# A long convolution and an MLP on one core: another order of issue, more buffers, reads and loads on other queues, half of y formed in the front, MLP rows turned by transfers

## The chip, the cores and the metric

One core of a Trainium2 chip runs the whole program. The metric is the device time of one execution in microseconds (us); lower is better. TensorE is PE (its weight loads PEld), VectorE is DVE, ScalarE is ACT, GpSimd is POOL and SyncE is SP. SP and POOL issue the transfers here; each takes its issues in the order of its program, and a wait of one holds up what stands behind it.

## What is computed

x is 2048 x 512 in bf16. A state-space layer filters the normed x along the 2048 rows, each of 512 channels with a filter of its own made from 128 complex modes (Uf and Kf are the spectra of the padded rows and filter); a layer norm, an MLP of width 1376 and two residual sums follow.

```python
def _A_ref(u, A_re, A_im, B_re, B_im, C_re, C_im, log_dt, Dskip):
    ...
    P = jnp.exp(logdA[:, :, None] * l[None, None, :])
    K = jnp.einsum("dn,dnl,dn->dl", Cc, P, dB).real
    ...
    Yf = Uf * Kf[None, :, :, :]
    ...
    y = y.transpose(0, 2, 1) + u * Dskip[None, None, :]
    return y

def _B_ref(x, w1, b1, w2, b2):
    y = _layernorm(x, axis=-1)
    h = _gelu(jnp.einsum("bsd,df->bsf", y, w1) + b1)
    return jnp.einsum("bsf,fd->bsd", h, w2) + b2

x = A_u
h = x + _A_ref(_layernorm(x, axis=-1), A_A_re, A_A_im, A_B_re, A_B_im, A_C_re, A_C_im, A_log_dt, A_Dskip)
h2 = h + _B_ref(_layernorm(h, axis=-1), B_w1, B_b1, B_w2, B_b2)
```

## The kernel before

The convolution is a Fourier product made of matmuls. In the **front**, the 16 row groups of x are normed (`norm_in`: statistics, then `roots`), and each goes through a first stage: `norm` makes `u`, two matmuls `aps`, a copy to the tile `a`, a write to `A_dram` (L786). Four loads (`x_load`, L798) bring that back in another layout as X, and `x_stage` multiplies X by the table M, in eight pairs for each half of the channels. Beside that `params`, `tables`, `exps`, `p_half`, `q_half` and `kgen` make the filter of one half of the channels (256): P and Q are phases (PE), sines (ACT) and products (DVE); `kgen` multiplies them in bursts of 128 matmuls of 20 columns (`kps`, L704), writes the filter to DRAM (`puts`, L729) and reads it back as `kt` (`gets`, L736: five reads, three of SP and two of POOL).

`conv` then goes over eight tiles k2 for a half: `spectrum` (four groups of five matmuls of 256 columns, L840, two of them led by one of two rows for the skip term, L838), a copy to `kf`, four DVE products, `back` (eight matmuls, L862 to 865), a copy to `z` (3 buffers), a write of 256 KB to `Zd` (the put, L883), and a read of it with rows and columns exchanged into `ZT` (the turned read, `turn`, L881). The second half does the same.

All of this is issued in an order written out as a list of numbers (`ORDER`): each operation of `Sched` has an index, an entry is twice the index plus the choice of engine where there are two, and every engine and queue takes its own in the order of the list. When both halves are in `ZT`, the **MLP** starts: y of a row group is two matmuls over `ZT` (by `Dm`), x is added, and `bn_stats` and `bn_aggr` give the norm. There are four tiles of four row groups. For each, `scale` norms the rows, `turn` transposes them on PE (`tps`, four 128 x 128 blocks a row group) and copies them with ACT to `y2T`, `up` runs 11 chunks of W1 with a gelu, and `down` 11 chunks of W2, adds the residual and stores. Tile 0 goes in two pairs of row groups. y of the next tile (`y_row`) stands between the up chunks, its transposes between the rows of `down`. `loads` brings W1, x and W2 from POOL in one go, once `kt` of the second half has landed: 1376, 512, 1280 and 1536 KB and some small ones. One part of y, the first half of the channels for the four rows of tile 0, is formed in the front (`early_rows`).

Of the kernel before, what the change touches and what calls it, by code (L numbers as in the profile page):

```python
# [915 lines left out]
def load_w1(nc, K, big, sb, w1, b1):  # L916
    both = big.tile([P, 4 * F + 4 * 512], bf16, name="w1_r0", tag="b2")
    K.w1_sb = both[:, 0:4 * F].rearrange("p (c f) -> p c f", c=4)
    K.r0 = both[:, 4 * F:].rearrange("p (j d) -> p j d", j=4)
    nc.gpsimd.dma_start(K.w1_sb, w1.rearrange("(dc p) f -> p dc f", p=P))  # L920
    b1_bf = sb.tile([P, NFC], bf16, name="b1_bf")
    nc.gpsimd.memset(b1_bf[:], 0.0)
    with nc.allow_non_contiguous_dma(reason="tiny bias load"):
        nc.gpsimd.dma_start(b1_bf[:, 0:10], b1[0:1280].rearrange("(fc p) -> p fc", p=P))
        nc.gpsimd.dma_start(b1_bf[0:96, 10:11], b1[1280:1376].rearrange("(p o) -> p o", o=1))
    K.b1_bf, K.b1_sb = b1_bf, sb.tile([P, NFC], f32, name="b1_sb")
# [9 lines left out]
def mlp(nc, tc, K, ZT, ov):  # L936
    with tc.tile_pool(name="m_sb", bufs=1) as sb, tc.tile_pool(name="m_rot", bufs=2) as rot, tc.tile_pool(name="m_ps", bufs=2, space=PSUM) as ps1:
        warm = sb.tile([1, 1], f32, name="warm")
        nc.scalar.activation(warm[:], K.ones[0:1, 0:1], ACT.Sqrt)
# [30 lines left out]
        def y_row(tb, jj):  # L970
            j = 4 * tb + jj
            yp = ps1.tile([P, 512], f32, name="yps")
            for h in range(2):
                nc.tensor.matmul(yp[:], lhsT=K.D[:, h], rhs=ZT[:, :, h, j, :], start=(h == 0), stop=(h == 1))  # L974
            st = rot.tile([P, 6], f32, name="st2")
            tt(nc, h_of(j), yp[:], K.r1[:, j - 4, :], ALU.add)
            nc.vector.bn_stats(st[:], h_of(j))
            nc.vector.bn_aggr(mv[tb][:, jj, :], st[:])

        def turn(tb, js):  # L980
# [29 lines left out]
        pairs = (slice(0, 2), slice(2, 4))  # L1010
        for n, js in enumerate(pairs):
            yp = yps[n] = ps1.tile([P, 2, HW], f32, name="y1", tag="yps")
            first_half(nc, K, yp, 1, js)
        tiles(1)
        at = {0: 0, 2: 1, 6: 2, 10: 3}
        for n, js in enumerate(pairs):
            first_sums(nc, K, yps[n][:], 1, js)
            for jj in range(js.start, js.stop):
# [149 lines left out]
```

## Time and profile before

| | |
|---|---|
| median of 3 runs | 339.08 us (338.14 to 341.11) |
| span of the profiled execution | 340.1 us |
| PE busy | 253.5 us, 75% |
| DVE busy | 203.8 us, 60% |
| ACT busy | 188.0 us, 55% |
| POOL busy | 32.6 us, 10% |
| moved by DMA | 30.18 MB, mean 89 GB/s |

The profile is of one execution. A busy time says how long an engine had an instruction in work; a wait is put down to what ended it last. A chain is followed back from the last instruction to what released each step, so its shares say which work or transfer set the end. The granted clock is that of TensorE as a share of full speed (1.00 is 2.4 GHz and 0.50 is 1.2 GHz). In the rows, starts are us from the start of the span, and several instructions of one kind in a row are merged (x2).

### The profile page before, as it was taken

What the parts mean: (1) busy time and instruction counts of PE and PEld (TensorE: products, weight loads), DVE (VectorE), ACT (ScalarE), POOL (GpSimd) and SP (SyncE); (2) the same over time, 40 slices, a digit from 0 to 9 for tenths busy, and PEclk for the clock granted to TensorE, in tenths of its full rate; (3) what the DMA queues carried; (4) which work ended last, traced back from release to release, by engine and by line L of the source; (5) the groups of instructions that cost most, each with busy time, mean ns of one, the idle gap of its engine ahead of it and who ended that gap; (6) DMA issues with size and microseconds to landing.
All of it is one profiled execution on the core that took longest, in us unless ns stands there. A gap on an engine that the chain in (4) does not pass through costs nothing.

```text
span 340.1 us, 6070 instructions
## 1 busy us (share of the span) xinstructions
PE 253.5 (75%) x2408; PEld 155.3 (46%) x2422; DVE 203.8 (60%) x427; ACT 188.0 (55%) x308; POOL 32.6 (10%) x92
## 2 busy tenths in 40 slices
PE   4046984476674998998798978502689799999996
PEld 4012351242373775667666755401465344444443
DVE  3999995559981999989224443510727367274102
ACT  2799796479832999986143525420573263363440
POOL 8200007800000100000015000100000000000000
PEclk9655567579955899999599997965599999999999
DMA  6400007640156921111098964443000100100001
GB/s 180 175 2 0 4 18 195 201 147 0 65 166 169 245 67 31 45 49 35 4 239 225 337 230 125 123 124 93 0 2 0 46 17 15 47 2 31 31 11 52
DMA packets 29830, 30.18 MB, mean 89 GB/s; under 512 B 7113, under 2 KB 27594, under 8 KB 29418
## 3 DMA queue, kind: packets, MB, share of 16 engines
q1 hardware_dynamic: 27722, 23.03, 23.4%
q0 software_dynamic: 2080, 6.76, 6.4%
q8 instruction: 19, 0.31, 0.4%
q14 instruction: 9, 0.07, 0.1%
HBM read 18.58 MB, written 11.20 MB: 88 GB/s over the span
## 4 chain that ended last, share of the span: by engine, by line
PE 36%; DMA 24%; DVE 18%; ACT 12%; issue 6%; POOL 2%; SPq 1%; DVEq 0%; ACTq 0%; POOLq 0%
DMA Zd<-z 13%; PE h1ps L992 12%; PE o2ps L1004 9%; PE kps L704 5%; DMA A_dram<-a 5%; PE kfps L840 4%; DMA kt<-KD_far 3%; DVE st L761 3%; DVE Pt L70 3%; DMA KD_far<-far 2%; DVE w L70 2%; ACT a L80 2%; PE yps L974 2%; ACT y2T L80 2%; DVE Q L70 1%
## 5 line engine op out<-in xcount | busy, mean ns | idle before, releaser
L994 ACT ACTIVATE hT<-h1ps,b_sb 128x512 bf16<-128x512 f32 (+3 forms) x55 | 33.0, 603 | 28.0 <-PE h1ps L992 27.4
L992 PE MATMUL h1ps<-y2T,w_r 128*128 128x512 bf16 (+3 forms) x217 | 44.7, 350 | 2.3 <-ACT y2T L80 1.9
L840 PE MATMUL kfps<-kt,M 128*128 128x256 bf16 x320 | 42.2, 278 | 1.2 <-DMA kt<-KD_far 0.6
L1004 PE MATMUL o2ps<-w_sb,hT 128*128 128x512 bf16 (+3 forms) x183 | 39.2, 366 | 1.7 <-DVE ot L70 1.5
L840 PEld LDWEIGHTS <-M 128*128 128x128 bf16 x320 | 29.2, 99 | 10.1 <-issue 3.4
L992 PEld LDWEIGHTS <-w_r 128*128 128x128 bf16 (+1 forms) x220 | 23.0, 105 | 22.4 <-issue 4.9
L70 DVE TENSOR_TENSOR pa<-X,kf 128x1024 bf16<-128x1024 bf16 x16 | 11.1, 691 | 28.1 <-ACT kf L80 28.1
L1004 PEld LDWEIGHTS <-hT 128*128 128x128 bf16 (+1 forms) x187 | 18.1, 98 | 20.9 <-issue 1.8
L704 PE MATMUL kps<-Q,Pt 128*32 128x20 bf16 x1024 | 18.6, 221 | 11.2 <-issue 9.6
L70 DVE TENSOR_TENSOR ot<-o2ps,h_sb 128x512 bf16<-128x512 f32 (+1 forms) x13 | 8.4, 650 | 29.6 <-PE o2ps L1004 28.7
L80 ACT CAST kf<-kfps 128x1024 bf16<-128x1024 f32 x14 | 14.2, 1013 | 17.2 <-PE kfps L840 9.0
L704 PEld LDWEIGHTS <-Pt 128*32 128x32 bf16 x1024 | 17.9, 169 | 12.4 <-issue 10.5
L80 ACT CAST z<-zps 128x1024 bf16<-128x1024 f32 x15 | 15.3, 1023 | 13.6 <-DMA Zd<-z 12.8
L80 ACT CAST a<-aps 128x1024 bf16<-128x1024 f32 x15 | 15.0, 1033 | 12.2 <-DMA A_dram<-a 12.2
L70 DVE TENSOR_TENSOR Pt<-s,Pt 128x1024 bf16<-128x1024 bf16 x32 | 20.4, 691 | 1.2 <-ACT s L118 1.1
L118 ACT ACTIVATE sq<-qv 128x1024 bf16<-128x1024 int16 x20 | 20.3, 1072 | 0.0
L613 ACT ACTIVATE Pt<-th 128x256 bf16<-128x256 f32 x64 | 20.3, 405 | 0.0
L80 ACT COPY y2T<-tps 128x512 bf16<-128x512 bf16 x16 | 8.5, 584 | 17.6 <-PE tps L984 17.6
L405 POOL DMA_DIRECT2D Dp<-Dd x24 | 13.0, 546 | 43.7 <-DMA Dd<-ds 42.1
L70 DVE TENSOR_TENSOR h_sb<-yps,r 128x512 f32<-128x512 f32 x12 | 8.3, 689 | 14.8 <-PE yps L974 14.8
L777 PE MATMUL aps<-u,BD 128*128 128x512 bf16 x30 | 11.0, 473 | 8.0 <-DVE u L772 5.3
L118 ACT ACTIVATE s<-pv 128x1024 bf16<-128x1024 int16 x16 | 16.6, 1064 | 0.0
(224 smaller groups left out, 470.9 us busy)
## 6 DMA issues: line engine op xcount, KB each, us to landing
A_dram<-a SPq DMA_DIRECT2D x16, 256.0 KB, 3.0
X<-A_dram SPq DMA_DIRECT2D x4, 1024.0 KB, 6.0
Zd<-z SPq DMA_DIRECT2D x16, 256.0 KB, 3.4
ZT<-Zd SPq DMA_DIRECT2D x16, 256.0 KB, 3.4
x<-in_A_u_dram SPq DMA_DIRECT2D x4, 512.0 KB, 8.7
out_dram<-ot SPq DMA_DIRECT2D x15, 128.0 KB, 1.7
r<-in_A_u_dram POOLq DMA_DIRECT2D x1, 1536.0 KB, 15.9
w_r<-in_B_w_dram POOLq DMA_DIRECT2D x1, 1376.0 KB, 8.6
```

The source lines that it names most:

```text
L70: nc.vector.tensor_tensor(out, a, b, op)
L80: nc.scalar.copy(out, in_)
L118: nc.scalar.activation(out, v.bitcast(i16)[..., 0:2 * n:2], ACT.Sin, scale=S2PI / 65536)
L405: nc.gpsimd.dma_start(t[o::128 // cnt], bass.AP(row.tensor, row.offset + 1024 * kh, [[0, cnt], [1, 1024]]))
L613: nc.scalar.activation(K.Pt[:, k, 1, :], K.th[:, ds], ACT.Exp, scale=float(8 * k))
L704: nc.tensor.matmul(kps[32 * g:32 * g + 32, i // 8, at:at + 20], lhsT=Pt[:, :, u, c], rhs=Q[:, :, u, c], start=True, stop=True, tile_positi ...
L761: o = S.op("DVE", 2.9, roots, deps=[S.op("DVE", 0.62, lambda j=j: nc.vector.bn_stats(st[:, j, :], x[:, j, :]), [here]) for j in range(16)])
L777: nc.tensor.matmul(ps[:, h, :], lhsT=K.BD[:, h].rearrange("p a b -> p (a b)"), rhs=cell["u"][:], start=True, stop=True)
L840: nc.tensor.matmul(ps[:, k, c, :], lhsT=K.M[:, t, 2 * k2 + k, c, :], rhs=kt[:, t, :], start=(c == 1 and t == 0), stop=(t == 4))
L992: nc.tensor.matmul(pt[:fs, 0:n], lhsT=K.w1_sb[:, dc, fc * P:fc * P + fs], rhs=y2T[tb][:, dc, js, :].rearrange("p a b -> p (a b)"), start=( ...
L994: nc.scalar.activation(hT[tb % 2][:fs, fc, cols], pt[:fs, 0:n], ACT.Gelu_apprx_tanh, bias=K.b1_sb[:fs, fc:fc + 1], scale=1.0)
L1004: nc.tensor.matmul(pt[:], lhsT=h[:fs, fc, jj * P:(jj + 1) * P], rhs=K.w2_sb[:fs, fc, d], start=(fc == 0), stop=(fc == NFC - 1))
```

## The change

- **Order.** The list is new: 537 entries where there were 522. In the front, operations of P and Q stand between the 16 rows; the sign, Q-by-amp products and last-row sums come behind `roots`, the Dirichlet sums and two pieces ahead of it. The first `X` load is issued behind all writes of `a` and ahead of the filter's puts. Eleven of the 16 products of `x_stage` stand behind the first spectrum, where there were eight. In `conv` nine of the 16 copies to `kf` are DVE's, where there were two.
- **Buffers.** `a` has 4 in place of 2.
- **Skip matmul.** `top` has 128 rows, zero but for two, and the skip term is a matmul with 128 rows of ones.
- **Queues.** All five reads of `kt` are SP's. A turned read can go to POOL or SP: three are POOL's (tiles 0 and 5 of half 0, tile 0 of half 1), 13 are SP's. The end of SP's list for half 1 reads: put 1; turns 7, 6 and 2 of half 0; put 0, turn 1, put 3, put 4, a piece of x, turn 4, put 5, put 2, put 6, turn 3, turn 2, put 7, turn 5, turn 6, turn 7.
- **Loads.** W1 comes in four pieces (three of POOL, one of SP) once `kgen` of half 1 is through, x in four pieces (one of POOL, three of SP), into the room of X that the products of half 0 have left; W2 is loaded at the start of the MLP, behind the `hT` memset.
- **Half of y in the front.** For all 16 rows, the first half of y is formed and summed in the front, in four groups of one matmul block and one DVE sum each; the MLP adds the second half.
- **MLP.** Tile 0 is still transposed on PE; for tiles 1 to 3 `scale` issues a transposing transfer from SP for each row, straight from `y2` to `y2T`.

```diff
-            (nc.gpsimd if t % 2 else nc.sync).dma_start(kt[:, t, :].rearrange("p (g c) -> p g c", g=4), src)
+            nc.sync.dma_start(kt[:, t, :].rearrange("p (g c) -> p g c", g=4), src)
...
-            cell["a"] = lp.tile([P, 2, 512], bf16, name="a", tag="a", bufs=2)
+            cell["a"] = lp.tile([P, 2, 512], bf16, name="a", tag="a", bufs=4)
...
-                        nc.tensor.matmul(ps[:, k, c, :], lhsT=K.ones[0:2, :], rhs=K.top[:, ds], start=True, stop=False)
+                        nc.tensor.matmul(ps[:, k, c, :], lhsT=K.ones[:], rhs=K.top[:, ds], start=True, stop=False)
...
-        def turn(k2=k2):
-            nc.sync.dma_start(K.ZT[k2:k2 + 121:8, hh].rearrange("p h j d -> p (h j d)"), Zd[4 * k2:4 * k2 + 4].rearrange("f (q r) d -> (f q) (r d)", q=4))
+        def turn(e, k2=k2):
+            (nc.sync if e == "SP" else nc.gpsimd).dma_start(K.ZT[k2:k2 + 121:8, hh].rearrange("p h j d -> p (h j d)"), Zd[4 * k2:4 * k2 + 4].rearrange("f (q r) d -> (f q) (r d)", q=4))
...
-def first_sums(nc, K, y, hh, js):
+def half_sums(nc, K, y, hh, js):
     ds = slice(HW * hh, HW * hh + HW)
-    tt(nc, K.h0[:, js, ds], y, K.r0[:, js, ds], ALU.add)
+    tt(nc, K.h[:, js, ds], y, K.X[:, js, hh, 0:HW], ALU.add)
     for j in range(js.start, js.stop):
-        nc.vector.bn_stats(K.st0[:, j, hh, :], K.h0[:, j, ds])
...
+        nc.vector.bn_stats(K.st[:, j, hh, :], K.h[:, j, ds])
+
+
+def early_rows(nc, S, K, psp, z0, r0):
+    for n in range(4):
+        cell = {}
+        js = slice(4 * n, 4 * n + 4)
+
+        def mm(cell=cell, js=js):
+            cell["y"] = psp.tile([P, 4, HW], f32, name="y0", tag="p", bufs=PB)
+            half_rows(nc, K, cell["y"], 0, js)
+
+        m = S.op("PE", 1.0, mm, z0, acq="p")
+        K.o_early.append(S.op("DVE", 2.8, lambda cell=cell, js=js: half_sums(nc, K, cell["y"][:], 0, js), [m, r0[n]], rel=[m]))
...
+    w1v = w1.rearrange("(dc p) f -> p dc f", p=P)
+    ends = []
+    for dc in range(4):
+        ends.append(S.op(("POOL", "SP"), (0.8, 0.45), lambda e, dc=dc: (nc.gpsimd if e == "POOL" else nc.sync).dma_start(K.w1_sb[:, dc], w1v[:, dc]), deps, lat=2.5))
...
         for n in range(2):
             nc.gpsimd.memset(hT[n][96:97, NFC - 1, :], 1.0)
+        load_w2(nc, K, sb, w2, b2)
...
-                ts(nc, y2[tb][:, jj, :], h_of(4 * tb + jj), mv[tb][:, jj, 0:1], ALU.subtract, rs[:, k:k + 1], ALU.mult)
+                ts(nc, y2[tb][:, jj, :], K.h[:, 4 * tb + jj, :], mv[tb][:, jj, 0:1], ALU.subtract, rs[:, k:k + 1], ALU.mult)
+                if tb:
+                    nc.sync.dma_start_transpose(y2T[tb][:, :, jj, :], y2[tb][:, jj, :])
...
+        def y_rows(tb, n):
+            yp = yps[tb, n] = ps1.tile([P, 2, HW], f32, name="y1", tag="yps")
+            half_rows(nc, K, yp, 1, slice(4 * tb + 2 * n, 4 * tb + 2 * n + 2))
+
+        def sums(tb, n):
+            half_sums(nc, K, yps[tb, n][:], 1, slice(4 * tb + 2 * n, 4 * tb + 2 * n + 2))
+            for jj in (2 * n, 2 * n + 1):
+                nc.vector.bn_aggr(mv[tb][:, jj, :], K.st[:, 4 * tb + jj].rearrange("p h s -> p (h s)"))
...
         for n, js in enumerate(pairs):
...
+            sums(0, n)
             scale(0, js)
-            turn(0, js)
+            turn(js)
+            y_rows(1, n)
             for fc in range(NFC):
                 up(0, fc, js)
-                if n and fc in at:
-                    y_row(1, at[fc])
+            sums(1, n)
         scale(1, slice(0, 4))
...
                     up(tb, fc, slice(0, 4))
-                    if tb < 3 and fc in (1, 3, 5, 7):
-                        y_row(tb + 1, fc // 2)
+                    if tb < 3 and fc in (1, 3):
+                        y_rows(tb + 1, fc // 2)
                 if tb < 3:
+                    for n in range(2):
+                        sums(tb + 1, n)
                     scale(tb + 1, slice(0, 4))
             for jj in range(4):
                 down(tb, jj)
-                if jj == (2 if tb == 0 else 1) and tb < 3:
-                    turn(tb + 1, slice(0, 4))
...
-    K.top = cp.tile([2, 512], bf16, name="top")
+    K.top = cp.tile([P, 512], bf16, name="top")
+    nc.gpsimd.memset(K.top[:], 0.0)
...
+    def residual(e, n):
+        (nc.gpsimd if e == "POOL" else nc.sync).dma_start(K.X[:, 4 * n:4 * n + 4, :, 0:HW], xv[:, 4 * n:4 * n + 4].rearrange("p j (h d) -> p j h d", h=2))
```

## Rows read from the trace of the kernel before

**Rows 1.** The page's part 4, the chain's shares of the span, by line.
```profile
DMA Zd<-z 13%; PE h1ps L992 12%; PE o2ps L1004 9%; PE kps L704 5%; DMA A_dram<-a 5%; PE kfps L840 4%; DMA kt<-KD_far 3%; DVE st L761 3%; DVE Pt L70 3%; DMA KD_far<-far 2%; DVE w L70 2%; ACT a L80 2%; PE yps L974 2%; ACT y2T L80 2%; DVE Q L70 1%
```

**Rows 2.** Windows: stretch, its length, each engine's busy us (instructions), PEclk, DMA share, GB/s.
```profile
43.10:109.30 66.20, 40.82 (x681) 25.15 (x684) 46.45 (x88) 42.02 (x50) 12.98 (x24) 0.71 0.41 121
118.20:218.50 100.30, 87.83 (x1100) 64.45 (x1104) 62.78 (x110) 59.88 (x82) 7.37 (x13) 0.93 0.44 128
218.50:242.30 23.80, 4.00 (x27) 2.56 (x26) 7.12 (x19) 5.13 (x8) 0.98 (x2) 0.59 0.32 88
242.30:340.10 97.80, 89.64 (x480) 46.82 (x486) 43.02 (x108) 40.30 (x69) 0.00 (x0) 0.97 0.06 22
```

**Rows 3.** Waits of ACT: engine, tile, line <- what ended it: us, times, longest.
```profile
ACT z L80 <- DMA Zd<-z: 12.8, 6, 5.0
ACT a L80 <- DMA A_dram<-a: 12.2, 9, 2.5
```

**Rows 4.** The same for SP's queue.
```profile
SPq L881 <- DMA Zd<-z: 41.5, 11, 11.4
```

**Rows 5.** Timeline of SP's queue at the end of the front: start, us, issue.
```profile
229.29 0.57 SPq L883 DMA_DIRECT2D Zd<-z  x1
232.83 0.48 SPq L881 DMA_DIRECT2D ZT<-Zd  x1
```

**Rows 6.** Timeline of DVE ahead of the roots.
```profile
34.69 2.49 DVE L624 TENSOR_TENSOR Q<-Q,amp 128x1024 bf16<-128x1024 bf16 x4
```

**Rows 7.** Timeline of PE in the second half's conv.
```profile
210.66 0.27 PE L862 MATMUL zps<-pa,R 128*128 128x256 bf16 x1
...
211.42 0.27 PE L865 MATMUL zps<-pa,R 128*128 128x256 bf16 x1
...
211.63 0.28 PE L838 MATMUL kfps<-top,ones 2*128 2x256 bf16 x1
...
213.04 0.28 PE L838 MATMUL kfps<-top,ones 2*128 2x256 bf16 x1
```

**Rows 8.** Timeline of PE in kgen of half 0.
```profile
100.75 2.32 PE L704 MATMUL kps<-Q,Pt 128*32 128x20 bf16 x128 [1.13 <-issue]
```

**Rows 9.** The page's part 5: group, count | busy us, mean ns | idle before, releaser.
```profile
L80 ACT CAST z<-zps 128x1024 bf16<-128x1024 f32 x15 | 15.3, 1023 | 13.6 <-DMA Zd<-z 12.8
```

**Rows 10.** Timeline of DVE, the early sum of four rows.
```profile
219.62 1.23 DVE L70 TENSOR_TENSOR h<-y,w_r 128x1024 f32<-128x1024 f32 x1 [1.89 <-PE y L890]
...
220.88 1.41 DVE L897 BATCH_NORM_STATS2 st<-h 128x6 f32<-128x256 f32 x4
```

**Rows 11.** Timeline of PE and DVE in the MLP.
```profile
265.23 2.54 PE L1004 MATMUL o2ps<-w_sb,hT 128*128 128x512 bf16 x11 [1.52 <-DVE ot L70]
...
267.61 0.61 PE L984 MATMUL tps<-ident,y 128*128 128x128 bf16 x8
...
269.38 2.54 PE L1004 MATMUL o2ps<-w_sb,hT 128*128 128x512 bf16 x10
...
302.59 0.59 PE L974 MATMUL yps<-ZT,Dm 128*128 128x512 bf16 x2
...
306.88 1.92 DVE L66 TENSOR_SCALAR y<-h_sb,mv,r4y 128x512 bf16<-128x512 f32 x4
...
317.08 10.32 PE L992 MATMUL h1ps<-y2T,w_r 128*128 128x512 bf16 x43
...
327.24 9.71 PE L1004 MATMUL o2ps<-w_sb,hT 128*128 128x512 bf16 x55
```

**Rows 12.** DMA issues: out<-in, queue, count, KB each, median us to landing.
```profile
out_dram<-ot SPq DMA_DIRECT2D x15, 128.0 KB, 1.7
...
w_sb<-in_B_w_dram POOLq DMA_DIRECT2D x1, 1280.0 KB, 12.3
Dp<-Dd POOLq DMA_DIRECT2D x8, 128.0 KB, 4.5
...
b_bf<-in_B_b_dram POOLq DMA_DIRECT2D x1, 2.5 KB, 7.8
```

More of the change, by code (lines that the diff above doesn't have):

```diff
@@ L455, in tr @@
                 T[nm] = ps[:, n, :]
-        arrive = S2("LOAD", 0.85, lambda: None, [arrive] if arrive is not None else [])
+        arrive = S2("LOAD", 0.85 if arrive is not None else 4.4, lambda: None, [arrive] if arrive is not None else [])
         Z[pair[0]] = S2("PE", 1.75, tr, [arrive], acq="p", bias=300)
@@ L735, in gets @@
             src = near[:].rearrange("(g k) r c -> (k r) g c", g=4)[128 * t:128 * t + 128] if t < 2 else far[t - 2].rearrange("(g k) r c -> (k r) g c", g=4)
-            (nc.gpsimd if t % 2 else nc.sync).dma_start(kt[:, t, :].rearrange("p (g c) -> p g c", g=4), src)
-    p = S.op("SP", 2.0, puts, ends, rel=[ends[0]], lat=3.0)
+            nc.sync.dma_start(kt[:, t, :].rearrange("p (g c) -> p g c", g=4), src)
+    p = K.o_put = S.op("SP", 2.0, puts, ends, rel=[ends[0]], lat=3.0)
     K.o_kt[hh] = S.op("SP", 1.0, gets, [p], lat=3.0, acq="kt")
@@ L826, in conv @@
     N = [P, 2, 2, HW]
-    K.o_z, back_ops = [], []
+    K.o_z, K.o_prod, back_ops = [], [], []
     for k2 in range(8):
@@ L874, in conv @@
         x = S.op("DVE", 2.1, prod, [f] + [K.o_x[hh][k2]], acq="pa", rel=[f], bias=-1.0 * k2)
+        K.o_prod.append(x)
         S.group = f"z{hh}"
@@ L878, in conv, with half_rows @@
         e = S.op(("ACT", "DVE"), (0.94, 1.2), zout, [z], acq="z", rel=[z], bias=-1.0 * k2)
-        def turn(k2=k2):
-            nc.sync.dma_start(K.ZT[k2:k2 + 121:8, hh].rearrange("p h j d -> p (h j d)"), Zd[4 * k2:4 * k2 + 4].rearrange("f (q r) d -> (f q) (r d)", q=4))
+        def turn(e, k2=k2):
+            (nc.sync if e == "SP" else nc.gpsimd).dma_start(K.ZT[k2:k2 + 121:8, hh].rearrange("p h j d -> p (h j d)"), Zd[4 * k2:4 * k2 + 4].rearrange("f (q r) d -> (f q) (r d)", q=4))
         w = S.op("SP", 0.45, lambda cell=cell, ks=ks: nc.sync.dma_start(Zd[2 * ks.start:2 * ks.stop].rearrange("f p d -> p f d"), cell["zs"][:].rearrange("p k c d -> p (k c) d")), [e], rel=[e], lat=2.4)
-        K.o_z.append(S.op("SP", 0.45, turn, [w, K.o_turn], lat=2.8))
-def first_half(nc, K, out, hh, js):
+        K.o_z.append(S.op(("SP", "POOL"), (0.45, 0.8), turn, [w, K.o_turn], lat=2.8))
+def half_rows(nc, K, out, hh, js):
     for j in range(js.start, js.stop):
@@ L913, with load_w1, biases @@
 FSZ = [128] * 10 + [96]
[L916 to L926, printed above, removed]
+def load_w1(nc, S, K, wl, sb, w1, b1, deps):
+    w1v = w1.rearrange("(dc p) f -> p dc f", p=P)
+    ends = []
+    for dc in range(4):
+        ends.append(S.op(("POOL", "SP"), (0.8, 0.45), lambda e, dc=dc: (nc.gpsimd if e == "POOL" else nc.sync).dma_start(K.w1_sb[:, dc], w1v[:, dc]), deps, lat=2.5))
+    def biases():
+        b1_bf = sb.tile([P, NFC], bf16, name="b1_bf")
+        nc.gpsimd.memset(b1_bf[:], 0.0)
+        with nc.allow_non_contiguous_dma(reason="tiny bias load"):
+            nc.gpsimd.dma_start(b1_bf[:, 0:10], b1[0:1280].rearrange("(fc p) -> p fc", p=P))
+            nc.gpsimd.dma_start(b1_bf[0:96, 10:11], b1[1280:1376].rearrange("(p o) -> p o", o=1))
+        K.b1_sb = sb.tile([P, NFC], f32, name="b1_sb")
+        nc.gpsimd.tensor_copy(K.b1_sb[:], b1_bf[:])
+    S.op("POOL", 4.0, biases, [])
+    return ends
 def load_w2(nc, K, sb, w2, b2):
@@ L939, in mlp @@
         nc.scalar.activation(warm[:], K.ones[0:1, 0:1], ACT.Sqrt)
-        h1_sb = sb.tile([P, 12, 512], f32, name="h1_sb")
-        def h_of(j):
-            return K.h0[:, j, :] if j < 4 else h1_sb[:, j - 4, :]
         hT = [sb.tile([P, NFC, 512], bf16, name=f"hT{n}") for n in range(2)]
@@ L968, in tiles, with turn @@
             y2T[tb] = rot.tile([P, 4, 4, P], bf16, name="y2T")
[L970 to L980, printed above, removed]
+        def y_rows(tb, n):
[5 more added lines that the diff above has]
+                nc.vector.bn_aggr(mv[tb][:, jj, :], K.st[:, 4 * tb + jj].rearrange("p h s -> p (h s)"))
+        def turn(js):
             for jj in range(js.start, js.stop):
@@ L983, in turn @@
                 for dc in range(4):
-                    nc.tensor.transpose(tp[:, dc, :], y2[tb][:, jj, dc * P:(dc + 1) * P], K.ident[:])
-                evac(nc, 0, y2T[tb][:, :, jj, :], tp[:])
+                    nc.tensor.transpose(tp[:, dc, :], y2[0][:, jj, dc * P:(dc + 1) * P], K.ident[:])
+                evac(nc, 0, y2T[0][:, :, jj, :], tp[:])
         def up(tb, fc, js):
@@ L1005, in down @@
                 ot = rot.tile([P, 512 // parts], bf16, name="ot", tag="ot")
-                tt(nc, ot[:], pt[:], h_of(j)[:, d], ALU.add)
+                tt(nc, ot[:], pt[:], K.h[:, j, d], ALU.add)
                 nc.sync.dma_start(ov[j][:, d], ot[:])
@@ L1010, in mlp @@
         pairs = (slice(0, 2), slice(2, 4))
+        for n in range(2):
+            y_rows(0, n)
+        tiles(1)
         for n, js in enumerate(pairs):
[L1012 to L1018, printed above, removed]
-                nc.vector.bn_aggr(mv[0][:, jj, :], K.st0[:, jj].rearrange("p h s -> p (h s)"))
+            sums(0, n)
             scale(0, js)
-            turn(0, js)
+            turn(js)
+            y_rows(1, n)
             for fc in range(NFC):
                 up(0, fc, js)
-                if n and fc in at:
-                    y_row(1, at[fc])
+            sums(1, n)
         scale(1, slice(0, 4))
@@ L1032, in mlp @@
                     up(tb, fc, slice(0, 4))
-                    if tb < 3 and fc in (1, 3, 5, 7):
-                        y_row(tb + 1, fc // 2)
+                    if tb < 3 and fc in (1, 3):
+                        y_rows(tb + 1, fc // 2)
                 if tb < 3:
+                    for n in range(2):
+                        sums(tb + 1, n)
                     scale(tb + 1, slice(0, 4))
@@ L1111, in turn, with tail @@
         K.ZT = big.tile([P, 2, 2, 16, HW], bf16, name="ZT", tag="b1")
-    def loads():
+        K.w1_sb = big.tile([P, 4, F], bf16, name="w1", tag="b2")
+    def tail():
         work.close()
         wl = ctx.enter_context(tc.tile_pool(name="wl", bufs=1, side="right"))
-        K.h0 = wl.tile([P, 4, 512], f32, name="h0")
-        K.st0 = wl.tile([P, 4, 2, 6], f32, name="st0")
-        gate = wl.tile([P, 1], bf16, name="gate")
-        nc.gpsimd.tensor_copy(gate[:], K.kt[1][:, 4, 0:1])
-        load_w1(nc, K, big, cp, B_w1, B_b1)
-        nc.gpsimd.dma_start(K.r0, xv[:, 0:4])
-        load_w2(nc, K, wl, B_w2, B_b2)
-        K.r1 = wl.tile([P, 12, 512], bf16, name="r1")
-        nc.gpsimd.dma_start(K.r1[:], xv[:, 4:16])
-        nc.gpsimd.tensor_copy(K.b1_sb[:], K.b1_bf[:])
+        K.h = wl.tile([P, 16, 512], f32, name="h")
+        K.st = wl.tile([P, 16, 2, 6], f32, name="st0")
+    def residual(e, n):
+        (nc.gpsimd if e == "POOL" else nc.sync).dma_start(K.X[:, 4 * n:4 * n + 4, :, 0:HW], xv[:, 4 * n:4 * n + 4].rearrange("p j (h d) -> p j h d", h=2))
     S.group = None
     K.o_turn = S.op("NONE", 0.0, turn, K.o_kgen)
-    ld = S.op("POOL", 6.0, loads, [K.o_kt[1]], lat=8.0)
+    load_w1(nc, S, K, None, cp, B_w1, B_b1, [K.o_turn])
+    o_tail = S.op("NONE", 0.0, tail, [K.o_put, K.o_turn])
     part("kf0", conv, cv, psp, Zd[0], 0)
-    z0 = K.o_z
+    z0, x0 = K.o_z, K.o_prod
     part("kf1", conv, cv, psp, Zd[1], 1)
-    part("first_rows", early_rows, psp, z0 + [ld] + K.o_z[6:7])
+    r0 = [S.op(("POOL", "SP"), (0.8, 0.45), lambda e, n=n: residual(e, n), x0[2 * n:2 * n + 2], lat=3.0) for n in range(4)]
+    K.o_early = []
+    part("early", early_rows, psp, z0 + [o_tail], r0)
     S.run(ORDER)
     front.close()
-    mlp(nc, tc, K, K.ZT, out_dram.rearrange("(p j) d -> j p d", j=16))
+    mlp(nc, tc, K, B_w2, B_b2, out_dram.rearrange("(p j) d -> j p d", j=16))
     order.__exit__(None, None, None)
```

11 lines of the change are left out of this document (2 added, 9 removed), and 32 rows, old and new, of the table ORDER.

## The prediction, made before the changed kernel was run

> **What bounds the kernel now.** I read the chain that ended last first. It is cut by line, and its largest line is no engine's: the write of z to DRAM, with more writes and reads of the same kind behind it [rows 1]. So time is lost where engines stand still for transfers. To see where, I cut the span at instructions that all later work needs, in us: A, to the end of the norm's roots, 43.1; B, to the last output of the first filter half (kgen of half 0), 109.3; C, to the first spectrum matmul, 118.2; D, to the last back matmul, 218.5; E, to the first up matmul of the MLP, 242.3; F, to the end, 340.1. The reader is to see how far each engine is from full in each [rows 2]: in B DVE works 46.5 of 66.2 and PE 40.8 at a mean clock of 0.71; in D PE works 87.8 of 100.3; in E nobody works; in F PE is nearly full.
>
> The waits name what B and D lose: ACT waits 12.2 in 9 waits for an `a` buffer whose write has not landed, and 12.8 in 6 for a `z` buffer [rows 3]. SyncE's own waits give the cause of the second: 41.5 ahead of the turned read (L881), for the put just before it, 11 times [rows 4]. In SP's timeline the last tiles go put, turn, put, turn, a put 3.5 behind the turn that follows it [rows 5], long after PE had done its part.
>
> The profiled span is 340.1 and the median of the runs 339.08, 1.0 below it. My sum goes by the span, and 1.0 is taken off at the end.
>
> **A** (43.1). DVE's list sets this end. Four products of Q by amp go behind the roots: 2.5 [rows 6]. The last-row sums go behind too, the Dirichlet sums and two pieces come ahead; I take these as even. A becomes 40.6 (bounds 39 and 43.1). First on POOL stands a memset of `top`, and SP's load of `top`, the last of its loads, waits for it; nothing needs it before C: hidden.
>
> **B** (66.2). Four `a` buffers stand in place of two, and p and q work is laid between the 16 rows. If DVE never stood, its 46.5 would be the length [rows 2]. The other bound is PE. Eight matmuls of 256 columns start 0.109 apart at full clock (210.66 to 211.42 is seven steps [rows 7]); 512 columns are 0.22, and 0.44 at half clock. PE's work in B after the change, all at half clock: 16 rows x 2 x 0.44 = 14.1; p 8 x 0.88 = 7.0; q 10 x 0.86 = 8.6; phases 28 x 0.44 = 12.3; 56 transposes 6.1; kgen 4 x 2.32 + 3 x 1.13 of issue [rows 8] = 12.7; in all 60.8. Between 46.5 and 60.8 I take the middle, 53.6: the mean clock of 0.71 in B is as near to one level as to the other.
>
> **C** (8.9). All five gets of `kt` are now SP's, where POOL had two: two more issues of 0.5, as a turn's [rows 5]. The first filter matmul waits for them; meanwhile ACT has the exps of half 1 and DVE its copies of X, as before. C becomes 9.9 (bounds 8.9 and 12).
>
> **D** (100.3). From one 2-row skip matmul to the next is 1.41 (211.63 to 213.04 [rows 7]); 11 matmuls at 0.109 are 1.20. So the 128-row form saves 0.21 x 32 = 6.7 of PE. PE's list before: 16 spectra x 2.82 = 45.1, 16 backs x 0.87 = 13.9, 8 X products x 0.87 = 7.0, p and q at full clock 8.1, kgen 12.7, y of four rows 0.9; 87.7, as the 87.8 of the table. After: spectra 38.4, backs 13.9, 11 X products 9.6 (three were in B and C), p and q 8.1, kgen 12.7, half of y for all 16 rows 3.5; 86.2. The stalls were 12.6. Those by z go where a put no longer stands behind a turn that waits; I let half of all go: D becomes 92.5 (bounds 86.2, no stall, and 100.3). DVE's list, 62.8 before, grows by seven copies of kf (8.6) and one early sum (2.6), some 75: covered.
>
> SP's order decides here. Of the second half's turns three stand near behind their put and ahead of other puts (tiles 1, 4 and 2); before, 11 waits were of this kind [rows 4]. Three turns are POOL's, and what waits behind them on POOL are pieces of W1 and x, wanted only in E. W1 and x go in four pieces each, where 4.7 MB were in flight at once and one put took 11.4 to land [rows 4], against 3.5 late [rows 5].
>
> **E** (23.8). Before, SP still had three puts and four turns to send after the last back matmul. After, it is the copy of z, 1.0 [rows 9], one put, 3.5, and from the issue of the last turn (232.83 [rows 5]) to the first up matmul (242.3) 9.4 as before: 13.9. Three of the four early sums now stand on DVE behind the last product: 1.23 + 1.41 each [rows 10], 7.9 in all; the copy and the put are 4.5, and a turn as long as a put, 3.5 more, covers the rest. New beside the put is W2: its load stands on POOL behind the `hT` memset, which waits for the last back matmul. 4.7 MB in flight made a put 7.9 longer (11.4 against 3.5); by bytes 1.4 MB make it 2.4 (bounds 0 and 7.9). E becomes 16.3.
>
> **F** (97.8). The transposes of tiles 1 to 3 leave PE and ACT: 267.61 to 269.38 is 1.77 for one tile [rows 11], 5.3 for three. Half of y for 12 rows went to D: 12 x 2 x 0.109 = 2.6. The wait of 1.5 for DVE (265.23 [rows 11]) goes, because DVE's sums are done sooner. That is 9.4. W2 took 12.3 to land [rows 12] and is wanted some 16 after the first up matmul: hidden; late by as much as it lands after that.
>
> Against it stand 12 transposing transfers on SP, which no row shows. An up stage takes 10.2 (317.08 to 327.24), y 0.9 and a down stage 9.7 [rows 11]: 20.8 to the next up, which needs all four. The second pair's y starts after four of eleven chunks, at 4.1; from there to the first row of y2 it was 4.3 (302.59 to 306.88 [rows 11]), now two rows at once, 4.5, and that row 0.5: 9.1. So four transfers have 11.7 together, 2.9 each if one follows the other. Nearest is the store of `ot`, 128 KB on the same queue, 1.7; farther are `Dp`, 128 KB, 4.5, and the load of `b1`, which moves two-byte elements one by one, 7.8 [rows 12]. Bounds: 0 and 3 x (4 x 7.8 - 11.7) = 58. By the nearest row they hide; for the smaller pieces I add 2.0. Stores of `ot` queue behind them, but their data come later. F becomes 90.4.
>
> The Trainium skill's page "VectorE: DVE Perf Modes", section "The three transpose paths", gives 1309 ns for a 128x128 block through the DMA crossbar; with four blocks a row, one after another, that would be an estimate of 5.2 a row, 28 late in all, a total near 328. Its page "Advanced Engine Details and Errata", section "X-Bar Transpose (TRN2)", says that such transfers are as fast as ordinary ones; by it the total would be near 300. No row here shows either.
>
> **Sum.** 40.6 + 53.6 + 9.9 + 92.5 + 16.3 + 90.4 = 303.3; less 1.0: 302.
>
> **Rivals.** First, the change does not do what it says: only 3 of 16 turned reads are on POOL, 13 stay in one line with the puts. If waits ahead of puts still hold the `z` buffers, D and E stay: 302 + 7.8 + 7.5 = 317. For it: three such waits are left, and the last put stands behind the turn of tile 2. Against it: three are not eleven, and other issues lie between a put and its turn. 0.16, 312 to 326.
>
> Second, a transposing transfer takes what `Dp` took, 4.5, one after another: 18 - 11.7 = 6.3 late a tile, 19 in all in place of 2: 319, from 312 to 338. For it: its pieces are small; against it: the 1.7 of the store. 0.12, of which 0.02 within 1% of before. The skill's 1309 ns would lie in this case.
>
> Third, on the other side: each takes 6.6 or more, toward `b1`'s 7.8. At 6.6 a tile is 14.7 late, 44 in all: 344, slower by 1.5%; at 7.8 it is 358. Below 6.5 it is not slower. For it: no row of such a transfer; against it: `b1` was loaded while megabytes of others were in flight, and in F only stores move. 0.08.
>
> The forecast, from 289 (B and D near their lower bounds) to 318 (PE at half clock in B, few stalls gone in D), has 0.58. Below 289 stand 0.02, and 0.04 between 326 and 342 by other ways, of which 0.03 within 1%.
>
> **How the numbers follow.** About 1%, 335.7 to 342.5, is what a measurement of this kernel can tell from no change. Faster: 0.58 + 0.16 + 0.10 + 0.02 + 0.01 = 0.87. Same: 0.02 + 0.03 = 0.05. Slower: 0.08. The range 288 to 328 holds the forecast (0.58), the first rival (0.16) and most of the second (0.08): 0.82.
>
> **What would show it.** B right: ACT's waits on A_dram under 2 in sum, and the last filter output near 95. D right: 1.2 a half spectrum, no idle ahead of L838, z waits under 4. E right: one put and one turn between the last back matmul and the y of the MLP. F right: no tps in tiles 1 to 3 and no wait of PE for `y2T`. Wrong would be: PE waiting on `y2T` for more than 3 a tile (second or third rival), SP waiting over 20 at L881 ahead of puts (first), or the clock at 0.5 all through B.

## The result, and the profile after

The changed kernel takes 301.56 us (median, 298.42 to 303.06) beside 338.61 of the kernel before; the ratio is 0.886, 95% interval 0.879 to 0.894. Ratios are of fast runs alone, and of these four one (303.06) counts as slow. In a second set of runs beside the experiments it took 301.40 (ratio 0.880, 0.877 to 0.883). Forecast were 302 and a range of 288 to 328.

The profiled execution has a span of 296.5 and a time of 298.4, the shortest of the four; that of the second set took 303.9, the longest of its six. Cut as in the prediction (the end of D is taken 0.2 later here, at the end of the last back matmul, in every kernel), with the profiled execution of the second set in the last column, in us:

| | before | forecast | after | after, again |
|---|---|---|---|---|
| A to the roots | 43.1 | 40.6 | 40.4 | 40.4 |
| B to the first filter half | 66.2 | 53.6 | 52.2 | 53.6 |
| C to the first spectrum | 8.9 | 9.9 | 11.5 | 11.5 |
| D to the last back matmul | 100.5 | 92.5 | 84.7 | 87.2 |
| E to the first up matmul | 23.6 | 16.3 | 19.4 | 20.7 |
| F to the end | 97.8 | 90.4 | 88.3 | 88.4 |
| span | 340.1 | 303.3 | 296.5 | 301.8 |

That the sum came out so near is in part luck: D was forecast 8 too long (5 in the second execution) and F 2, which stands against C and E, 2 and 3 to 4 too short. The steps are taken apart below. First the windows of after, B to F, which answer to [rows 2]: stretch, length, each engine's busy us (instructions), PEclk, DMA share, GB/s.

```profile
core 0: us, PE busy (x) PEld busy (x) DVE busy (x) ACT busy (x) POOL busy (x), PEclk, DMA share, GB/s
40.40:92.60 52.20, 43.49 (x666) 23.38 (x669) 46.26 (x85) 43.06 (x51) 0.00 (x0) 0.73 0.31 103
92.60:104.10 11.50, 7.20 (x54) 5.42 (x53) 10.74 (x16) 11.49 (x37) 0.00 (x0) 0.85 0.79 199
104.10:188.80 84.70, 83.36 (x1156) 71.27 (x1159) 73.68 (x122) 52.16 (x68) 4.12 (x7) 1.00 0.54 149
188.80:208.20 19.40, 3.70 (x20) 2.40 (x21) 9.43 (x23) 5.13 (x8) 2.96 (x5) 0.57 0.67 158
208.20:296.50 88.30, 83.52 (x429) 43.17 (x434) 36.24 (x106) 33.87 (x57) 0.00 (x0) 0.98 0.17 43
```

B: DVE works the same 46 as before, but in 52 and not in 66. D: PE works 83.4 of 84.7, so it is now the bound. E is still a stretch in which nobody works. The waits of SP's queue (engine, line <- what ended it: us, times, longest) and of PE in D answer to [rows 4]:

```profile
SPq L882 <- DMA Zd<-z: 3.0, 2, 1.6
...
PE kfps L838 <- DVE X L82: 1.3, 1, 1.3
PE pv L643 <- ACT sq L118: 0.5, 1, 0.5
PE kps L704 <- issue: 0.5, 1, 0.5
```

The 41.5 in which SP stood ahead of turned reads are 3.0, and no other row names a `z` write any more, but POOL's with its own turned reads, which hold nobody up. In E, the timelines of SP, POOL and PE (start, us, issue or instruction, idle before it) answer to [rows 5]:

```profile
189.87 0.36 SPq L884 DMA_DIRECT2D Zd<-z  x1
190.34 3.04 SPq L882 DMA_DIRECT2D ZT<-Zd  x3
...
189.80 1.00 POOL L940 DMA_DIRECT2D w_sb<-in_B_w_dram  x1
...
202.25 1.87 PE L891 MATMUL y<-ZT,Dm 128*128 128x256 bf16 x8 [13.49 <-DMA ZT<-Zd]
```

The last put and three turned reads stand behind the last back matmul, and the last of the three is that put's, as the prediction has it; W2's load starts beside them. The last read was issued at 192.9, and the y matmuls that wait for it start at 202.25, 9.3 later. The five turned reads issued from 187.7 on landed after (min/median/max):

```profile
DMA to landing us min/median/max: 3.6/5.9/8.9
```

In F, the first transposed tile on SP, the up stage that reads it on PE, and the DMA issues of the transfers (count, median us to landing):

```profile
221.21 5.24 SPq L970 DMA_TRANSPOSE y2T<-y  x4
...
233.17 1.68 PE L998 MATMUL h1ps<-y2T,w 128*128 128x512 bf16 x7
...
y2T<-y SPq DMA_TRANSPOSE x12, 2.4
```

Four transfers leave SP in 5.24, the last of them at 225.2, and each lands 2.4 after its issue; the up stage starts at 233.17 without a wait, 5.6 after the last has landed.

### The profile page after: what moved, and what is told of

It reads as the page before. It is cut to its first block, busy times and chain, and to the rows that moved or that the text cites. A ratio compares the mean times of both kernels' runs of the same rounds, so it can differ in the third digit from the quotient of the medians.

```text
span 296.5 us, 6029 instructions
## 1 busy us (share of the span) xinstructions
PE 237.6 (80%) x2383; PEld 154.9 (52%) x2398; DVE 210.5 (71%) x445; ACT 177.5 (60%) x289; POOL 31.3 (11%) x92
## 4 chain that ended last, share of the span: by engine, by line
PE 61%; ACT 14%; DVE 13%; DMA 5%; issue 4%; POOL 2%; ACTq 0%; DVEq 0%; POOLq 0%
PE h1ps L998 14%; PE o2ps L1010 12%; PE kfps L840 10%; PE kps L704 6%; ACT Pt L613 3%; DVE st L761 3%; DMA ZT<-Zd 3%; PE y L891 2%; ACT sq L118 2%; DVE w L70 2%; PE v L329 2%; ACT Q L620 2%; PE qv L676 2%; PE aps L777 2%; PE pv L643 2%
## 5 line engine op out<-in xcount | busy, mean ns | idle before, releaser
L998 PE MATMUL h1ps<-y2T,w 128*128 128x512 bf16 (+3 forms) x217 | 44.0, 347 | 1.4 <-ACT y2T L80 0.6
L70 DVE TENSOR_TENSOR ot<-o2ps,h 128x512 bf16<-128x512 f32 (+1 forms) x17 | 11.2, 660 | 41.7 <-PE o2ps L1010 40.3
L840 PE MATMUL kfps<-kt,M 128*128 128x256 bf16 x320 | 39.2, 273 | 0.0
L840 PEld LDWEIGHTS <-M 128*128 128x128 bf16 x320 | 31.3, 98 | 5.3 <-issue 1.4
L998 PEld LDWEIGHTS <-w 128*128 128x128 bf16 (+1 forms) x220 | 22.7, 103 | 21.2 <-issue 5.6
L70 DVE TENSOR_TENSOR h<-y,X 128x512 f32<-128x512 f32 (+1 forms) x12 | 10.3, 861 | 15.7 <-PE y L891 15.7
L891 PE MATMUL y<-ZT,Dm 128*128 128x256 bf16 x64 | 9.9, 300 | 13.5 <-DMA ZT<-Zd 13.5
L118 ACT ACTIVATE s<-pv 128x1024 bf16<-128x1024 int16 x16 | 16.3, 1044 | 2.5 <-DVE Pt L70 1.8
L891 PEld LDWEIGHTS <-Dm 128*128 128x128 bf16 x64 | 6.7, 106 | 15.7 <-issue 13.7
L517 PE MATMUL lps<-ident,M 128*128 128x128 bf16 x48 | 4.2, 257 | 12.5 <-DVE M L70 12.3
L643 PE MATMUL pv<-RP,PL 128*128 128x512 bf16 x29 | 11.0, 466 | 4.0 <-DVE r1t L70 2.8
## 6 DMA issues: line engine op xcount, KB each, us to landing
w_sb<-in_B_w_dram POOLq DMA_DIRECT2D x1, 1280.0 KB, 12.9
```

What stands on the lines that cost most here:

```text
L70: nc.vector.tensor_tensor(out, a, b, op)
L118: nc.scalar.activation(out, v.bitcast(i16)[..., 0:2 * n:2], ACT.Sin, scale=S2PI / 65536)
L643: nc.tensor.matmul(v[:, n], lhsT=K.PL[:, b, :], rhs=K.RP[:, 8 * n:8 * n + 8].rearrange("p i c d -> p (i c d)"), start=True, stop=True)
L840: nc.tensor.matmul(ps[:, k, c, :], lhsT=K.M[:, t, 2 * k2 + k, c, :], rhs=kt[:, t, :], start=(c == 1 and t == 0), stop=(t == 4))
L891: nc.tensor.matmul(out[:, j - js.start], lhsT=K.D[:, h], rhs=K.ZT[:, hh, h, j, :], start=(h == 0), stop=(h == 1))
L998: nc.tensor.matmul(pt[:fs, 0:n], lhsT=K.w1_sb[:, dc, fc * P:fc * P + fs], rhs=y2T[tb][:, dc, js, :].rearrange("p a b -> p (a b)"), start=( ...
```

## The experiments

Each is the kernel before with one or two parts of the change, or the changed kernel with one part undone or altered. Ratios are to the kernel before in the same set of runs (341.72, 342.17 and 343.29 us there), with 95% intervals.

### B: the buffers and the order

```diff
-cell["a"] = lp.tile([P, 2, 512], bf16, name="a", tag="a", bufs=2)
+cell["a"] = lp.tile([P, 2, 512], bf16, name="a", tag="a", bufs=4)
```

> The kernel before with one change: four a buffers in place of two, its order untouched. Theory (the buffers alone free B): ACT's wait of 12.2 for A_dram falls under 3 and most of it comes off stretch B (66.2): 327 to 331 us. Rival (the new order of p and q work between the rows did it): ACT then waits for something else, B loses under 3: 335 to 339 us.

334.65 us, ratio 0.980 (0.977 to 0.982), between the two forecasts; B 59.3. The other way round, in the changed kernel (`bufs=4` to 2, and in `ORDER` each write to A_dram behind its eviction):

> The changed kernel with two a buffers, the write of each row to A_dram standing right behind its eviction in SP's order (with the order as it was, two buffers can't be dealt out). In the kernel before four buffers alone took 6.8 of the 14 from B. Theory (the rest of B is the order's, and it needs the buffers): B from 52 to 59 or more, ACT waits over 6 for A_dram, 308 to 316 us. Rival (the order alone keeps ACT from standing): B 52 to 54, waits under 2, 300 to 304 us.

304.48 us, ratio 0.889 (0.885 to 0.893), against 0.880 of the changed kernel beside it; B 56.0. ACT's waits for A_dram in B, first the one, then the other:

```profile
ACT a L80 <- DMA A_dram<-a: 3.1, 2, 2.4
```
```profile
ACT a L80 <- DMA A_dram<-a: 0.7, 1, 0.7
```

Buffers alone take 6.9 from B (66.2), the order with two buffers 10.2, both 12.6 to 14.0. So they are two cures of one wait, and they don't add up: with p and q work between the rows (and each write right behind its eviction) the writes have landed before their buffer is wanted. Not all of the order's 10.2 is that wait: kgen's waits for nothing that the profile names ("issue") sum to 6.5 in B before, to 6.3 with four buffers alone, and to 3.2 in the changed kernel with two. My theory that the order needs the buffers fell. In the new order they are worth 3.1 by the medians (304.48 and 301.40); B's 2.4 in the profiles (56.0 to 53.6) shows nothing by itself, since B runs from 52.0 to 55.5 in executions of kernels that differ from the changed one only elsewhere.

### D: the skip matmul and SP's order

```diff
-nc.tensor.matmul(ps[:, k, c, :], lhsT=K.ones[0:2, :], rhs=K.top[:, ds], start=True, stop=False)
+nc.tensor.matmul(ps[:, k, c, :], lhsT=K.ones[:], rhs=K.top[:, ds], start=True, stop=False)
```

> The kernel before with one change: the skip matmul reads 128 rows (ones and zeros) in place of 2. Theory (the price is TensorE's and on the path): a half spectrum takes 1.20 in place of 1.41, and 6.7 comes off D: about 332 us. Rival (in the second half SP's line of puts and turned reads sets the pace, so what PE saves is given back as waits for z): half spectra 1.20, but 336 to 339 us.

339.68 us, ratio 0.995 (0.992 to 0.999); D 99.0. Waits of PE in D, ACT's for z, and the window of D:

```profile
PE zps L862 <- ACT z L80: 7.6, 4, 3.6
...
ACT z L80 <- DMA Zd<-z: 15.9, 6, 4.8
...
117.00:216.00 99.00, 83.43 (x1105) 68.06 (x1105) 62.54 (x110) 59.59 (x83) 7.34 (x13) 0.90 0.46 132
```

PE's busy time in D falls from 88.0 to 83.4, by 4.6 and not by 6.7, since the granted clock is 0.90 there and was 0.93; and its waits for z grow from 3.3 to 7.6, ACT's from 12.8 to 15.9. What PE saves goes into waits for puts, and some of it to the clock. The rival holds in the kernel before, if 0.7 above its range. In the changed kernel, the same edit undone:

> The changed kernel with one part undone: the skip matmul reads 2 rows again. Theory (in the changed kernel PE is the bound of D: it stood 1.3 of 84.5, so the whole 0.21 x 32 comes back): D 91, total 307 to 310 us. Rival (as in the kernel before, where this edit alone was worth 1.3 in D, PE's time is taken from waits): D 85 to 87, 302 to 305 us.

310.28 us, ratio 0.904 (0.896 to 0.913); D 92.3. PE's timeline in it:

```profile
192.21 0.27 PE L865 MATMUL zps<-pa,R 128*128 128x256 bf16 x1
192.42 0.28 PE L838 MATMUL kfps<-top,ones 2*128 2x256 bf16 x1
192.63 1.27 PE L840 MATMUL kfps<-kt,M 128*128 128x256 bf16 x10
```

The 2-row matmul stands 0.21 behind its neighbour and 0.21 ahead of the next, where others stand 0.11 apart; D is 5.1 to 7.6 longer than in the two executions of the changed kernel, 6.7 were expected. The other 2 to 3 of the total's 8.8 stand in B, which the edit doesn't touch: 55.5, at a granted clock of 0.68 beside 0.73 and 0.75. One edit, worth 1.5 in one kernel and the whole of its price in the other. What hid it was to be SP's order:

> The kernel before with one change: in SP's order each turned read of the second half stands behind the put of the tile two later (the last two behind the last put). Theory (a put that stands behind a waiting turned read holds the z buffers): SP's wait of 41.5 at L881 ahead of puts falls under 15, ACT's wait of 12.8 for z under 4, D loses 6 to 12 and E 3 to 7: 322 to 330 us. Rival (puts and reads are late because the transfers themselves are slow among 4.7 MB of loads): waits stay over 8, 334 to 339 us.

332.33 us, ratio 0.973 (0.968 to 0.978); D 99.2, E 13.6. SP's wait ahead of turned reads, and PE's wait in E, which was 16.6 in the kernel before:

```profile
SPq L881 <- DMA Zd<-z: 18.6, 5, 12.9
...
PE y L890 <- DMA ZT<-Zd: 6.6, 1, 6.6
```

So the order gives 10 in E, where 3 to 7 were expected, and 1.3 in D, where I had put 6 to 12; SP's wait didn't fall under 15. The time lies in the range of neither. Undone in the changed kernel (all 16 turned reads SP's, those of the second half behind their own put):

> The changed kernel with SP's order of before for the turned reads: those of the second half stand each right behind its own put, and all 16 are SP's. Theory (SP's order holds z buffers and delays the last tiles): SP waits over 15 at L882 ahead of puts, ACT waits for z buffers, D grows by 4 to 8, E by 2 to 6: 307 to 315 us. Rival (with four a buffers and the lighter spectra the waits don't reach PE): D and E within 2, 300 to 304 us.

312.06 us, ratio 0.911 (0.904 to 0.918); D 87.7, E 28.7. The end of SP's queue:

```profile
204.26 0.48 SPq L882 DMA_DIRECT2D ZT<-Zd  x1
204.83 0.53 SPq L884 DMA_DIRECT2D Zd<-z  x1
208.29 0.48 SPq L882 DMA_DIRECT2D ZT<-Zd  x1
208.87 0.53 SPq L884 DMA_DIRECT2D Zd<-z  x1
212.33 0.48 SPq L882 DMA_DIRECT2D ZT<-Zd  x1
```

The last back matmul ended at 193.2, yet SP still sends a pair every 4.0, up to 212.3. PE doesn't notice in D: the pairs fall behind, and the debt is paid in E. So the total is the theory's, but its split isn't: 4 to 8 were expected in D and 2 to 6 in E. Both together in the kernel before:

> The kernel before with two changes together: the turned reads of the second half two puts later, and the skip matmul of 128 rows. Alone they took 1.3 each from D (100.5 to 99.2 and 99.0). Theory (each hides the other: with the z buffers free PE is the bound of D, so the skip's 6.7 shows): D 91 to 93.5, E near 13.6, 322 to 326 us. Rival (D waits for DVE's products and ACT's evictions as the old order has them): D 96 to 98, 328 to 331 us.

328.17 us, ratio 0.953 (0.948 to 0.958); D 96.8, E 13.8. PE's waits in D and ACT's for z:

```profile
PE zps L862 <- ACT z L80: 5.8, 2, 3.1
...
ACT z L80 <- DMA Zd<-z: 8.5, 2, 4.7
```

D loses 3.7 where each alone lost 1.3 and 1.5: a little more than their sum, not the 7 to 9.5 of the theory. The sizes are the rival's, the cause isn't: PE still waits for z. All of ACT's 8.5 falls between 191 and 202. The put issued at 182.40, its time to landing, what SP sent next, and ACT's copies of z:

```profile
Zd<-z SPq DMA_DIRECT2D x1, 256.0 KB, 12.7
...
195.07 0.48 SPq L881 DMA_DIRECT2D ZT<-Zd  x1
195.64 2.88 SPq L883 DMA_DIRECT2D Zd<-z  x3
...
195.13 1.01 ACT L80 CAST z<-zps 128x1024 bf16<-128x1024 f32 x1 [3.81 <-DMA Zd<-z]
...
201.71 1.01 ACT L80 CAST z<-zps 128x1024 bf16<-128x1024 f32 x1 [4.65 <-DMA Zd<-z]
```

That put took 12.7 with the loads of W1, x and W2 (4.7 MB, issued at once from 178.8) in flight beside it; the four puts issued from 205 to 217 took 2.3 (median). ACT's first wait ends as it lands. The second is for puts that stood behind the last turned read of the first half, which this edit left in place and which waited 12.3 for the same put. So the put that is slow beside the loads holds the z buffers here, and the turned read that waits for it on SP passes the delay on to the puts behind. The changed kernel sends the loads in pieces; no run tests that part alone.

### E: W2 beside the last reads

```diff
+gate = sb.tile([P, 1], bf16, name="gate")
+nc.gpsimd.tensor_copy(gate[:], K.ZT[:, 1, 1, 15, HW - 1:HW])
 load_w2(nc, K, sb, w2, b2)
```

> The changed kernel, with the load of W2 held on POOL behind a copy of one column of ZT, so that it starts when the last turned read has landed. Theory (W2's 1.4 MB beside them makes the last turned reads slow): the last lands 3.3 to 4.5 after its issue, not 8.9, E falls from 19.6 to 14 to 15.5, W2 lands before the first down matmul: 296 to 298 us. Rival 1 (the five turned reads and puts in flight slow each other): E stays within 1 of 19.6, 300 to 303 us. Rival 2 (W2 comes too late for the first down stage): E falls, PE waits for w_sb in F, 300 us or more.

295.70 us, ratio 0.864 (0.858 to 0.871), so faster than the changed kernel; E 14.1. The copy on POOL, the y matmuls on PE, and W2's issue:

```profile
198.27 0.19 POOL L953 COPY gate<-ZT 128x1 bf16<-128x1 bf16 x1 [7.03 <-DMA ZT<-Zd]
...
198.29 1.87 PE L891 MATMUL y<-ZT,Dm 128*128 128x256 bf16 x8 [8.15 <-DMA ZT<-Zd]
...
w_sb<-in_B_w_dram POOLq DMA_DIRECT2D x1, 1280.0 KB, 7.1
```

The y matmuls start 3.9 after the last turned read's issue, not 9.3, and the five last reads (min/median/max) show the same:

```profile
DMA to landing us min/median/max: 3.6/4.0/4.5
```

The load itself takes 7.1, not 12.9: the two had slowed each other. W2 is there before the first down matmul, and F stays at 88.1.

On top of it, three of the four early y groups moved in `ORDER` on PE from among the last back matmuls to behind them:

> The changed kernel with W2's load behind the last turned read, and three of the four early y matmul groups moved on PE from among the last back matmuls to behind them, into the time in which PE stands in E. Theory (PE is the bound of D, E waits for the last turned read): D loses 3 x 0.9 = 2.6, E stays at 14.1, 290 to 294 us. Rival (their sums then end last, on DVE): three sums of 2.6 from about 189 end near 197, before the last read lands, so this would need the sums to start over 1.5 later; then 294 to 298 us.

295.56 us, ratio 0.860 (0.857 to 0.863), 0.981 of the changed kernel's 301.40 beside it. D 87.1, E 14.1: W2's gain is there, that of the move isn't.

```profile
190.77 0.28 PE L862 MATMUL zps<-pa,R 128*128 128x256 bf16 x1 [1.39 <-DVE pa L70]
```

Where the y groups had stood, PE now waits for DVE's product (1.6 in all). They had filled that gap, so PE's saving of 2.6 there bought little; the time is the rival's, but its cause (sums late on DVE) is not, since E is as short as without the move. This is the fastest version; of its two edits only W2's is shown to pay. The changed kernel in the same set:

> The changed kernel as it is, beside the others on their chip. Every theory: 0.886 of the kernel before, 300 to 304 us, D 84 to 87.5, E near 19.5, F near 88.

301.40 us, D 87.2, E 20.7, F 88.4, as expected.

### F: the transposing transfers

Undone (the `tps` transposes for tiles 1 to 3 back between the down groups, the transfers gone):

> The changed kernel with one part undone: tiles 1 to 3 are transposed by PE and evicted by ACT again, between the down groups. Theory (PE is the bound of F and the transposing transfers are hidden): 1.77 for each of three tiles comes back, F from 88.3 to 93 to 94: 306 to 308 us. Rival (the transfers cost PE or the stores as much as they save): within 2 of the changed kernel, 300 to 303 us.

306.98 us, ratio 0.897 (0.889 to 0.906); F 93.9, 5.6 longer. And tripled:

```diff
-nc.sync.dma_start_transpose(y2T[tb][:, :, jj, :], y2[tb][:, jj, :])
+for dst in (spare[0], spare[1], y2T[tb]):
+    nc.sync.dma_start_transpose(dst[:, :, jj, :], y2[tb][:, jj, :])
```

> The changed kernel with each transposing transfer issued three times, two of them into spare tiles that nobody reads, ahead of the real one. It tells the price of one and the slack left. Theory (SP's issue of 1.25 each is the whole price, one after another; the last lands about 4.3 before the up stage wants it): eight more are 10.0, less 4.3 is 5.7 late for each of three tiles: 17 more, 314 to 321 us. Rival 1 (the transfers share 16 engines and their issue is not the limit): within 3 of the changed kernel, 300 to 305 us. Rival 2 (each costs 5.2 of the transfer engines): 41.6 less 4.3 late, three times: over 400 us.

325.76 us, ratio 0.952 (0.945 to 0.959); F 111.0, 22.7 longer. SP's queue, PE's wait for y2T, and PE's timeline behind the first:

```profile
225.39 2.63 SPq L972 DMA_TRANSPOSE spare<-y  x2
228.07 1.26 SPq L972 DMA_TRANSPOSE y2T<-y  x1
...
PE h1ps L1000 <- DMA y2T<-y: 16.5, 3, 5.9
...
242.48 3.57 PE L1000 MATMUL h1ps<-y2T,w 128*128 128x512 bf16 x8 [4.96 <-DMA y2T<-y]
```

The wait is 5.5 a tile (5.7 was expected). From the first issue of a tile to the last is 14.5 in place of 4.0, so eight more cost 10.5, 1.3 each, one after another; less the slack of 5.6 that is 4.9, as the row shows for the first tile (the expectation had put each at 1.25 and the slack at 4.3). The other 6.2 of the 22.7 is the clock (PE works 89.5 in F, 5.9 more than in the changed kernel): after a wait eight matmuls of 512 columns take 3.57 where they take 1.89 in the changed kernel (253.28 there), and F's mean granted clock is 0.90, not 0.98. Rival 1 and rival 2 fall.

## Why the prediction was right, step by step

**A** was right (40.4 for 40.6): four products of Q out of DVE's list.

**B** was right in size (52.2 and 53.6 for 53.6), and its marks came: the last filter output at 92.6, no row of ACT waiting for A_dram. The clock lay between the levels as taken (0.73). That buffers and order each do most of the work was not in it; the sum named both and didn't need to tell them apart. That the middle of two bounds came out is luck in part: neither engine was full, with DVE at 46.3 and PE at 43.5 of 52.2.

**C** was too short by 1.6. The step priced two more gets on SP, but the first spectrum waits 1.3 for DVE's copy of X, in the PE waits above; in the second execution, with the same 11.5, an X product ahead of it waits 2.5 for such a copy. DVE works 10.7 of the 11.5 there, 7.6 of 8.9 before [rows 2], and its rows in C (group, count | busy, mean ns | idle before) show with what:

```profile
L82 DVE CAST X<-xps 128x1024 bf16<-128x1024 f32 x3 | 3.6, 1215 | 0.0
...
L70 DVE TENSOR_TENSOR M<-base,Dp 128x1024 bf16<-128x1024 bf16 x4 | 2.5, 684 | 0.0
L82 DVE COPY R<-rps 128x1024 bf16<-128x1024 bf16 x3 | 2.1, 684 | 0.8 <-PE rps L432 0.8
```

The prediction had DVE at "its copies of X, as before". They became fewer (three for six); the products for M, the copies of R and three more products of Q are work that came into C with the new order. No run tests this. A step that prices a reordering must count what arrives in the stretch, not only what leaves it.

**D** was too long by 8 (5 in the second execution). Two terms failed. First, the list of PE's work came to the table's 87.8 by luck. "kgen 12.7" counts three waits of 1.13 [rows 8] as work, though a wait is in no busy time; what stood in their place was the clock, which the list takes as full. Windows of the kernel before, then of the changed kernel's second execution, the last its whole D:

```profile
161.50:171.70 10.20, 7.94 (x294) 6.83 (x290) 2.02 (x6) 2.35 (x4) 0.00 (x0) 0.50 0.16 49
205.90:209.30 3.40, 3.40 (x16) 1.78 (x14) 2.06 (x4) 1.35 (x2) 0.00 (x0) 0.51 0.27 77
...
144.00:149.30 5.30, 5.30 (x40) 3.77 (x33) 2.63 (x6) 1.44 (x2) 2.54 (x4) 0.50 0.67 177
105.50:192.70 87.20, 85.89 (x1158) 72.49 (x1159) 73.74 (x122) 52.16 (x68) 4.10 (x7) 0.96 0.53 146
```

In the kernel before, the clock went to its lower level twice in D, first behind kgen's bursts with their waits. In the first execution of the changed kernel it stayed at 1.00, and PE worked 83.4: the bound of 86.2, less the 3.4 of waits, is 82.8. In the second it was at 0.50 up to 149.3, behind kgen again, and PE's work of 85.9 in place of 83.4 is the whole difference between the two. Of kgen's waits 0.5 is left in D; why they shrank with the order is not settled, and no run here tests it.

Second, "half of all stalls go": nearly all went; PE stands 1.3 of 84.7. The step gave as their cause that a put stands behind a waiting turned read. The runs show that this is not what D hung on: with that order back D is 87.7, and in the kernel before the new order on SP took 1.3 from D. What else freed D is open: the early y groups fill PE's waits for products (1.6 with three of them moved, in a_best); the loads in pieces and the copies of kf that went to DVE are parts that no run takes alone. The 6.7 of the skip was right, but only because PE had become the bound; alone it was worth 1.5.

**E** was too short by 3.1. Its form was right: the last put and its turned read stand behind the last back matmul (the read issued 4.1 behind it for 4.5), and undoing SP's order lengthens E by 8 to 9. The term that was mis-sized is W2's: 2.4 by bytes, measured 5.3 to 6.6 (19.4 and 20.7 less 14.1), inside its bounds of 0 to 7.9.

**F** was right: 9.5 gained, where the terms summed to 9.4 less 2.0. The transposes' 5.3 is 5.6 when undone; the 2.0 set against it for the transfers is 0. The slack of 11.7 for four was right too: from the first issue to the last landing they took 6.4 (221.2 to 227.6), and 5.6 was left.

The Trainium skill's page "VectorE: DVE Perf Modes", section "The three transpose paths", gives 1309 ns for a 128x128 block. Here a row of four blocks costs 1.3 of the queue and lands after 2.4, and eight more a tile cost 5.5 of waiting; so the measurement stands against an estimate of 5.2 a row, four blocks one after another. The Trainium skill's page "Advanced Engine Details and Errata", section "X-Bar Transpose (TRN2)", has them as fast as ordinary transfers: nearer, with 2.4 beside the 1.7 of a store of the same 128 KB [rows 12].

**The rivals.** The first (317: waits ahead of puts stay) would have shown as 20 or more at L882; it is 3.0. a_near builds that rival and took 312, but most of it in E and not in D. The second and third (a transfer of 4.5, of 6.6) fall with 1.3 a transfer; a_thrice, in which the real one stands behind two others, took 326 and shows the mechanism at work.

## What to carry to other kernels

Price an edit at the bound that holds once the other edits are in: the same 6.7 us of PE time was worth 1.5 while waits for puts set the pace and all of it when PE did. Two cures for one wait don't add up, and an order that lets a queue fall behind may cost nothing until the stage ends, where the whole debt falls due. Before the reads that end a stage, look at what else is put in flight: holding one load back until they had landed gave another 2%.
